# One of six additions of each convolution chunk moved from GpSimd to an accumulating DMA

## The chip, the core and the metric

The kernel runs on one core of a Trainium2 chip. A core has TensorE (matrix products into PSUM), VectorE, ScalarE and GpSimd (element-wise work), SyncE (here it only issues transfers) and 16 DMA engines that all issuers share. The metric is the device time of one execution in microseconds; the profile is of one execution.

## The reference

There are 8 batches of 4224 rows of 192 features. Each row has, for each of 8 heads, 7 raw tap weights. The reference (shortened):

```python
w = exp(weight_gen - max(weight_gen)); w = w / (sum(w) + 1e-9)   # softmax over the 7 taps
out[b, s, h, :] = sum_k w[b, s, h, k] * x_pad[b, s + k, h, :]    # causal, 6 rows of zeros ahead
X = fft(fft(out, axis=1), axis=2)
u = out + real(X)
un = (u - mean(u)) / sqrt(var(u) + 1e-6)
result = u + maximum(un @ w_ch1, 0) @ w_ch2                      # 192 -> 768 -> 192
```

So each batch goes through a dynamic convolution, a two-dimensional Fourier transform whose real part is added, a normalization and a two-layer network.

## The kernel before

The 4224 rows of a batch lie as 128 partitions x 33 row groups. A batch passes through four stages, each a Python generator that issues a little work per step:

- `conv(b)` (lines 306 to 487) computes the convolution in 8 chunks of 4 row groups (128 x 768 values, 384 KB, in f32) and a ninth chunk of one row group. For each chunk, each of the 7 taps gives a product of x and the tap's weight (line 440 on VectorE). The product of the first step (i == 0) is written to the sum `u` itself; the other six go to buffers `pr` (tag `prod`, 5 buffers) and are added to `u` one after the other. From the third batch on all six additions are on GpSimd (lines 448 and 449: `DVE_ADDS` names chunks of the second batch only, and `PE_SUMS` chunks of the first). GpSimd then folds the chunk (L463, L465, tile `sm`), TensorE multiplies it with Fourier tables (L470, `pg`), ScalarE and VectorE make `gt` of that, and SyncE stores it in DRAM (L484, L485, `g_d`).
- `transform(b)` loads `g_d` back (L506, tile `g2`, shown as g) and TensorE makes the second part of the transform (L516, `pp`), which ScalarE copies to `pq`.
- `mix(b, g)` multiplies `pq` with the feature tables (L545, `eo`); VectorE adds the result to `u` (L551 to L555). `norm(b, g)` normalizes a group on ScalarE (L585 to L600, tiles `junk`, `rs`, `un`; a small `rs` step on GpSimd, L598), splits it into a high f16 half (L608, ScalarE) and a low one (L609 and L611, GpSimd), the tile `hl`, and SyncE transposes that by DMA into `ht` (L617).
- `mlp(n)` runs the network for a group: five matmuls for each of six blocks of the hidden layer (L642, `ph`, three PSUM buffers), the rectified result as high and low halves `hh` (L652 on ScalarE, L653 on VectorE), and the second layer (L665, `po`). VectorE adds the residual (L670) and SyncE stores the result (L674).

The stages of different batches overlap: the streams' start and end times in `run()` let the convolution of batch b pass while the network of batch b - 1 and the one before still run. Each engine has one queue and works it in order. The order within a queue is set when the program is built: a planner with a model of the machine takes, on each engine, the work that is ready first, with the program order as priority; `issue_after` adds bounds on it. Once built, an instruction that waits holds everything behind it on its engine. SyncE issues every transfer of this kernel; x has one buffer, so the loads of the next batch (L326) wait for the products of this one.

Buffers matter for the change: a `pr` buffer is free again when the addition that reads it is done.

Of the kernel before, what the change touches and what calls it, by code (L numbers as in the profile page):

```python
# [14 lines left out]
ALU = mybir.AluOpType  # L15
# [21 lines left out]
POOL_TAPS = {(0, 0): (5, 6), (0, 1): (5, 6), (0, 3): (6,), (1, 0): range(7), (1, 1): range(7)}  # L37
DVE_ADDS = {(1, c): 1 for c in range(2, NC)}
F32_GROUPS = 7
ACT_TAPS = {(0, 1): (0,), (0, 3): (0,), (0, 5): (0,1), (0, 7): (0,)}  # L40
TURNS = {1: 'ddpdddd', 2: 'dpddpdd', 3: 'dpddpdp'}
WARM = (20, 0, 12, 12)
# [48 lines left out]
def tile_dynconv_fnet_mlp(  # L91
# [12 lines left out]
    nc = tc.nc  # L104
    B, D = x.shape[0], x.shape[3]
    H, K = wg.shape[3], wg.shape[4]
# [190 lines left out]
    def turns(pool, turn):  # L297

        its = {"p": iter(pool), "d": (k for k in range(K) if k not in pool)}
        return [next(its[t]) for t in turn]  # L300

    def mirrored(ap, step):

        return bass.AP(ap.tensor, ap.offset, [ap.ap[0], [step, 2], *ap.ap[1:]])

    def conv(b):
# [43 lines left out]
        for grp in groups:  # L350
            chunks = []
            wbank = wbanks[b] if b > 0 else pst("wp", 1, [P, 512], F32, f"wp_{b}_{grp[0]}")
            for i, c in enumerate(grp):
                need_x(c)
                need_taps(c)
                R = 4 if c < NC else 1
                on_pe = (b, c) in PE_SUMS
                u = us[b, c] = sb.tile([P, R, D], F32, name=f"u_{b}_{c}",
                                       **(dict(tag="u", bufs=16) if R > 1 else dict(tag="u0", bufs=2)))
# [9 lines left out]
                elif R > 1:  # L369
                    wout = wp.rearrange("p (s n) k -> p s n k", s=2)  # L370
                    nc.vector.tensor_tensor(out=wout, in0=win,
                                            in1=nin.unsqueeze(3).broadcast_to([P, 2, 2 * H, K]), op=ALU.mult)
                else:
                    nc.vector.tensor_tensor(out=wp, in0=w_sb[:, 0:H, :],
                                            in1=ws[:, 0:H].unsqueeze(2).broadcast_to([P, H, K]), op=ALU.mult)
                wq = None
                if len(pt) == K:
                    nc.vector.tensor_tensor(out=win, in0=win, in1=nin.unsqueeze(3).broadcast_to([P, 2, 2 * H, K]),
                                            op=ALU.mult)
                    wq = win  # L380
                elif pt:
                    wq = sb.tile([P, 2, 2 * H, len(pt)], F32, tag="wq", name=f"wq_{b}_{c}", bufs=2)
                    (nc.vector if c > 1 else nc.gpsimd).tensor_tensor(
                        out=wq, in0=win[:, :, :, pt[0]:pt[-1] + 1], in1=nin.unsqueeze(3).broadcast_to([P, 2, 2 * H, len(pt)]), op=ALU.mult)
# [8 lines left out]
            for c, R, u, wp, pa, wq, pt, at in chunks:  # L393
                act_taps = ACT_TAPS.get((b, c), ())
                if act_taps:
                    lo, up, n = 2 * c + 1, N2 - 2 * c - 2, len(act_taps)
                    step = (up - lo) * H
                    wa = sb.tile([P, 2, 2 * H, n], F32, tag="hh", name=f"wa_{b}_{c}", bufs=10)
                    wrows, nrows = w_sb[:, lo * H:(lo + 2) * H, :], ws_of[c][:, lo * H:(lo + 2) * H]
                    nc.vector.tensor_tensor(out=wa, in0=mirrored(wrows, step * K)[:, :, :, act_taps[0]:act_taps[0] + n],  # L400
                                            in1=mirrored(nrows, step).unsqueeze(3).broadcast_to([P, 2, 2 * H, n]), op=ALU.mult)
                for k in act_taps:
                    at[k] = [sb.tile([P, 2, D], F32, tag="hh", name=f"pr_{b}_{c}_{k}_{s}", bufs=10) for s in range(2)]
                    for s in range(2):
                        for j in range(2):
                            for h in range(H):
                                cols = slice(h * G, (h + 1) * G)
                                nc.scalar.mul(at[k][s][:, j, cols], x_sb[:, (up + K - 1 if s else lo) + j + k, cols],
                                              wa[:, s, j * H + h, k - act_taps[0]:k - act_taps[0] + 1])
            for i in range(K):  # L410
                for c, R, u, wp, pa, wq, pt, at in chunks:
                    order = turns(pt, TURNS[len(pt)]) if pt and pa else range(K)
                    order = [k for k in order if k not in at] + list(at)
                    k = order[i]
                    if k in at:
                        for h in range(2):
                            nc.tensor.matmul(pa[h][:, 0:2 * D], lhsT=ident32, rhs=at[k][h].rearrange("p r d -> p (r d)"),
                                             start=(i == 0), stop=(i == K - 1))
                        continue
                    pr = u  # L420
                    if i > 0 or pa:
                        pr = sb.tile([P, R, D], F32, name=f"pr_{b}_{c}_{k}",
                                     **(dict(tag="g2", bufs=3) if b == 0 and pa else dict(tag="prod", bufs=5)))
                    if R > 1:
                        lo, up = 2 * c + 1, N2 - 2 * c - 2 + K - 1
                        rows = mirrored(x_sb[:, lo + k:lo + k + 2, :].rearrange("p r (h g) -> p (r h) g", g=G),
                                        (up - lo) * D)
                        wk = wp[:, :, k:k + 1].rearrange("p (s n) o -> p s n o", s=2)
                        if k in pt:
                            wk = wq[:, :, :, k - pt[0]:k - pt[0] + 1]  # L430
                        wk = wk.broadcast_to([P, 2, 2 * H, G])
                        dst = pr.rearrange("p (s r) (h g) -> p s (r h) g", s=2, g=G)
                    else:
                        rows = x_sb[:, k, :].rearrange("p (h g) -> p h g", g=G)
                        wk = wp[:, :, k:k + 1].broadcast_to([P, H, G])
                        dst = pr.rearrange("p r (h g) -> p (r h) g", g=G)
                    if k in pt:
                        nc.gpsimd.tensor_tensor(out=dst, in0=rows, in1=wk, op=ALU.mult)
                    else:
                        last_product[b] = nc.vector.tensor_tensor(out=dst, in0=rows, in1=wk, op=ALU.mult)  # L440
                    if pa:
                        prf = pr.rearrange("p r d -> p (r d)")
                        n = R * D // 2
                        for h in range(2):
                            nc.tensor.matmul(pa[h][:, 0:n], lhsT=ident32, rhs=prf[:, h * n:(h + 1) * n],  # L445
                                             start=(i == 0), stop=(i == K - 1))
                    elif i > 0:
                        adder = nc.vector if i <= DVE_ADDS.get((b, c), 0) else nc.gpsimd
                        adder.tensor_tensor(out=u, in0=u, in1=pr, op=ALU.add)  # L449
                yield (done + sum(q[1] for q in tails) + sum(q[1] for q in chunks) * i / K) / N2  # L450
            tails += chunks
            while tails and not (b == 1 and grp[0] == 0):
                c, R, u, wp, pa, _, _, _ = tails.pop(0)
# [7 lines left out]
                if R > 1:  # L461
                    sm = sb.tile([P, 2, D], F32, tag="fold", name=f"sm_{b}_{c}", bufs=3)
                    nc.gpsimd.tensor_tensor(out=sm[:, :, 1:D], in0=u[:, 0:2, 1:D], in1=u[:, 3:1:-1, D - 1:0:-1],  # L463
                                            op=ALU.add)
                    last_fold[b] = nc.gpsimd.tensor_tensor(out=sm[:, :, 0], in0=u[:, 0:2, 0], in1=u[:, 3:1:-1, 0],  # L465
                                                           op=ALU.add)
# [155 lines left out]
    def mlp(n):  # L622
# [13 lines left out]
        for c in range(NH):  # L636
            if now:
# [3 lines left out]
                for i, (wt, blk) in enumerate(terms):  # L641
                    last_ph[n] = nc.tensor.matmul(ph[:, 0:T], lhsT=wt[:, cs_], rhs=ht[:, 0:T, blk],  # L642
                                                  start=(i == 0), stop=(i == len(terms) - 1))
                    if i < len(terms) - 1:
                        yield (c + 0.1 * (i + 1)) / NH
                if NG * b + g < F32_GROUPS:
                    a, l = sb.tile([P, 4, P], F32, tag="hh", name=f"hh_{b}_{g}_{c}", bufs=10), None
# [10 lines left out]
            if last:  # L658
                f32 = NG * lb + lg < F32_GROUPS
                per = LT  # L660
# [158 lines left out]
```

## Time and profile before

| | |
|---|---|
| median of 3 runs | 1142.97 us (1142.65 to 1143.59) |
| the profiled execution | 1139.56 us |
| its span, first to last instruction | 1137.8 us |
| mean granted TensorE clock | 0.988 |
| busy: TensorE, VectorE, ScalarE, GpSimd | 1077.1, 972.5, 811.1, 875.2 us |
| additions of line 449 on GpSimd | 396, of these 324 from the third batch on |
| moved by DMA | 128.74 MB, 113 GB/s in the mean |

In the rows PE is TensorE (PEld its weight loads), DVE VectorE, ACT ScalarE, POOL GpSimd and SP SyncE. A group has its busy time in us and the mean duration of one in ns, then the idle time of the engine just before them and what ended it. L449 is line 449 of the kernel. Instructions that issue a DMA do not count as busy. Times inside the execution are counted from the start of the span; in the third batch (b = 2 in the code, which counts from 0) the additions begin at 219 us, and the last batch's end at 961 us.

### The profile page before, as it was taken

Reading aid. Unit: us, or ns where it says so; the run is one execution under the profiler, and the core shown is the slowest. Engines: PE = TensorE matmul, PEld = TensorE weight load, DVE = VectorE, ACT = ScalarE, POOL = GpSimd, SP = SyncE. Lnnn points to the kernel's source line nnn. Section 1 sums busy time; section 2 is a strip of 40 time slices with the busy share of each in tenths; the row PEclk is TensorE's granted clock in tenths of the full one; section 3 lists DMA queues with packets and bytes.
Section 4 is the critical chain, followed back from the end, with each engine's and each line's share of the span. In section 5 each row is a group of like instructions: output and inputs, shape, how many; then the busy total and the mean of one; then the engine's idle time right before and its main releaser. Section 6 shows DMA issues by size and latency. Waiting matters only on the chain.

```text
span 1137.8 us, 23793 instructions
## 1 busy us (share of the span) xinstructions
PE 1077.1 (95%) x8476; PEld 815.0 (72%) x8476; DVE 972.5 (85%) x1825; ACT 811.1 (71%) x2520; POOL 875.2 (77%) x751
## 2 busy tenths in 40 slices
PE   5984999998999999999999999999999999999998
PEld 3454687786677867777778877677777867887777
DVE  7989999889989998999989998999989997356443
ACT  4665676456985799659975899559875898589822
POOL 5979699699978999699969999699959998011200
PEclk9996999999999999999999999999999999999999
DMA  8343344513483148514572347415562234421321
GB/s 304 129 151 98 64 115 134 171 39 113 96 214 103 54 115 228 133 53 120 137 177 81 103 97 216 129 36 129 141 156 60 65 73 98 115 57 46 85 46 47
DMA packets 156504, 128.74 MB, mean 113 GB/s; under 512 B 108571, under 2 KB 133088, under 8 KB 156384
## 3 DMA queue, kind: packets, MB, share of 16 engines
q1 hardware_dynamic: 156384, 127.21, 41.7%
q8 instruction: 67, 1.10, 0.4%
q14 instruction: 53, 0.43, 0.1%
HBM read 61.46 MB, written 39.37 MB: 89 GB/s over the span
## 4 chain that ended last, share of the span: by engine, by line
PE 45%; DVE 17%; ACT 14%; POOL 10%; issue 8%; DMA 5%; SPq 0%; DVEq 0%; POOLq 0%; ACTq 0%
PE ph L642 20%; PE po L665 17%; POOL u L449 7%; DVE pr L440 6%; PE pp L516 4%; ACT junk L589 3%; PE eo L545 2%; ACT junk L585 2%; DVE hh L653 2%; ACT un L600 2%; DMA ht<-hl 2%; ACT hh L652 2%; PE pg L470 1%; PE pa L445 1%; DVE u L440 1%
## 5 line engine op out<-in xcount | busy, mean ns | idle before, releaser
L449 POOL TENSOR_TENSOR u<-u,pr 128x768 f32<-128x768 f32 (+1 forms) x396 | 655.5, 1677 | 67.1 <-DVE pr L440 50.8
L665 PEld LDWEIGHTS <-hh 128*128 128x128 f16 x4248 | 362.7, 98 | 72.2 <-DVE hh L653 2.8
L665 PE MATMUL po<-w2h,hh 128*128 128x192 f16 x2832 | 408.4, 246 | 1.9 <-DVE hh L653 1.8
L642 PE MATMUL ph<-ht,w1h 128*128 128x512 f16 (+1 forms) x1296 | 394.4, 362 | 11.5 <-DMA ht<-hl 9.7
L440 DVE TENSOR_TENSOR pr<-x_sb,wp 128x768 f32<-128x768 f32 (+1 forms) x415 | 354.3, 877 | 14.1 <-POOL u L449 10.0
L665 PE MATMUL po<-w2l,hh 128*128 128x192 f16 x1416 | 345.4, 246 | 0.0
L653 DVE SCALAR_TENSOR_TENSOR hh<-ph,hh 128x512 f16<-128x512 f32 (+1 forms) x390 | 245.8, 636 | 106.4 <-ACT hh L652 105.5
L642 PE MATMUL ph<-ht,w1l 128*128 128x512 f16 (+1 forms) x864 | 310.2, 362 | 0.0
L652 ACT ACTIVATE hh<-ph 128x512 f16<-128x512 f32 (+1 forms) x390 | 213.8, 550 | 130.5 <-PE ph L642 101.7
L642 PEld LDWEIGHTS <-w1h 128*128 128x128 f16 x1296 | 125.5, 98 | 92.6 <-DMA ht<-hl 2.0
L600 ACT ACTIVATE un<-u,rs 128x192 f32<-128x192 f32 x264 | 123.7, 535 | 17.2 <-POOL rs L598 6.7
L642 PEld LDWEIGHTS <-w1l 128*128 128x128 f16 x864 | 85.2, 99 | 61.6 <-issue 11.8
L609 POOL TENSOR_TENSOR hl<-un,hl 128x512 f16<-128x512 f32 (+1 forms) x69 | 74.1, 1075 | 62.0 <-issue 28.8
L589 ACT ACTIVATE junk<-u,rs 128x192 f16<-128x192 f32 x244 | 110.3, 452 | 4.0
L585 ACT ACTIVATE junk<-u 128x192 f16<-128x192 f32 x244 | 88.0, 361 | 19.4 <-DVE u L555 15.9
L520 ACT COPY pq<-pp 97x204 f32<-97x204 f32 (+1 forms) x96 | 47.1, 491 | 58.0 <-PE pp L516 48.7
L545 PE MATMUL eo<-cs_sb,pq 97*128 97x97 f32 x544 | 82.4, 275 | 5.6 <-DVE u L555 5.6
L545 PEld LDWEIGHTS eo<-cs_sb,pq 97*128 97x128 f32 x544 | 76.7, 193 | 11.2 <-issue 6.9
L670 DVE SCALAR_TENSOR_TENSOR u<-po,isc,u 128x384 f32<-128x384 f32 (+1 forms) x122 | 72.6, 596 | 7.5 <-PE po L665 7.5
L463 POOL TENSOR_TENSOR sm<-u 128x382 f32<-128x382 f32 x64 | 65.6, 1025 | 5.0 <-ACT u L458 4.9
L665 PE MATMUL po<-w2f,hh 128*128 128x192 f32 x336 | 62.4, 327 | 0.0
L665 PEld LDWEIGHTS po<-w2f,hh 128*128 128x128 f32 x336 | 56.0, 190 | 4.6 <-PE pg L470 0.2
(111 smaller groups left out, 1265.4 us busy)
## 6 DMA issues: line engine op xcount, KB each, us to landing
out_dram<-u SPq DMA_DIRECT2D x64, 384.0 KB
x_sb<-in_x_dram SPq DMA_DIRECT2D x48, 384.0 KB
g<-g_d SPq DMA_DIRECT2D x40, 336.0 KB
x_sb<-in_x_dram SPq DMA_DIRECT2D x8, 864.0 KB
g_d<-gt SPq DMA_DIRECT2D x32, 195.0 KB
g_d<-gt SPq DMA_DIRECT2D x32, 189.0 KB
w<-in_weight_gen_dram SPq DMA_DIRECT2D x6, 924.0 KB
x_sb<-in_x_dram SPq DMA_DIRECT2D x8, 672.0 KB
```

Source lines behind the costliest of these rows:

```text
L440: last_product[b] = nc.vector.tensor_tensor(out=dst, in0=rows, in1=wk, op=ALU.mult)
L449: adder.tensor_tensor(out=u, in0=u, in1=pr, op=ALU.add)
L545: nc.tensor.matmul(eo[:, e, j, :], lhsT=pq[0:DH, e, r, r:r + P], rhs=cs_sb[:, e, :], start=True, stop=True)
L585: nc.scalar.activation(junk, uv[:, t, :], AF.Identity, accum_out=st[:, t, 0:1])
L589: nc.scalar.activation(junk, uv[:, t, :], AF.Square, bias=rs[:, 2, t:t + 1], accum_out=st[:, t, 1:2])
L600: nc.scalar.activation(halves[t // 2][:, t % 2, :], uv[:, t, :], AF.Identity, bias=rs[:, 1, t:t + 1], scale=rs[:, 0, t:t + 1])
L609: lo_eng.tensor_tensor(out=hl[:, t0:t1, 2 * P:3 * P], in0=src[:, 0:t1 - t0, 0:P], in1=hl[:, t0:t1, 0:P], op=ALU.subtract)
L642: last_ph[n] = nc.tensor.matmul(ph[:, 0:T], lhsT=wt[:, cs_], rhs=ht[:, 0:T, blk], start=(i == 0), stop=(i == len(terms) - 1))
L652: nc.scalar.activation(a[:, 0:T], ph[:, 0:T], AF.Relu)
L653: nc.vector.scalar_tensor_tensor(out=l[:, 0:T], in0=ph[:, 0:T], scalar=0.0, in1=a[:, 0:T], op0=ALU.max, op1=ALU.subtract)
L665: nc.tensor.matmul(po[t // 2][:, t % 2, :], lhsT=hx[:, t], rhs=wx[:, c2, :], start=(c2 == 0 and i == 0), stop=(c2 == NH - 1 and i == len(t ...
L670: nc.vector.scalar_tensor_tensor(out=lt, in0=po[t // 2][:, 0:t % 2 + 1], scalar=scales[0][:, 1:2] if f32 else isc, in1=lt, op0=ALU.mult, o ...
```

## The change

From the third batch on (`DMA_SUMS = 2`), in the eight chunks of four row groups, the products of steps 1 and 2 are no longer added to `u` as they come. They are kept as a pair, and when the second is there GpSimd issues a DMA that reads the second product and adds it to the first, in place, SBUF to SBUF (128 x 768 f32, 384 KB). At the last step, before the last product is added, GpSimd adds the pair's sum to `u`. So a chunk has five additions on GpSimd and one DMA where it had six additions. The ninth chunk and the first two batches are as before.

```diff
+DMA_SUMS = 2
...
+            pair = {}
             for i in range(K):
                 for c, R, u, wp, pa, wq, pt, at in chunks:
...
+                    elif R > 1 and b >= DMA_SUMS and i in (1, 2):
+                        pair.setdefault(c, []).append(pr)
+                        if i == 2:
+                            first, second = pair[c]
+                            nc.gpsimd.dma_start(first, second, accum_op=ALU.add)
                     elif i > 0:
+                        if c in pair and i == K - 1:
+                            nc.gpsimd.tensor_tensor(out=u, in0=u, in1=pair.pop(c)[0], op=ALU.add)
                         adder = nc.vector if i <= DVE_ADDS.get((b, c), 0) else nc.gpsimd
                         adder.tensor_tensor(out=u, in0=u, in1=pr, op=ALU.add)
```

## The prediction

> **What bounds the kernel now.** I read first the page's busy shares, then the chain that ended last.
>
> ```profile
> PE 1077.1 (95%) x8476; PEld 815.0 (72%) x8476; DVE 972.5 (85%) x1825; ACT 811.1 (71%) x2520; POOL 875.2 (77%) x751
> ...
> PE 45%; DVE 17%; ACT 14%; POOL 10%; issue 8%; DMA 5%; SPq 0%; DVEq 0%; POOLq 0%; ACTq 0%
> ```
>
> These are averages over stages, so the second view is the busy time by stretch: from the first addition of the third batch (b=2, about 219 us) to the last addition of the eighth (961 us), then one batch period, then ten busy microseconds of DMA. Columns: stretch, length, busy time of PE, PEld, DVE, ACT, POOL (with instruction counts), granted clock, DMA share, GB/s.
>
> ```profile
> 214.00:961.00 747.00, 726.88 (x6080) 558.03 (x6079) 698.63 (x1267) 571.57 (x1761) 680.04 (x576) 1.00 0.44 114
> 466.00:592.00 126.00, 124.44 (x1059) 95.80 (x1058) 119.79 (x212) 97.86 (x303) 113.97 (x97) 1.00 0.46 124
> 440.00:450.00 10.00, 10.00 (x83) 7.46 (x82) 7.87 (x22) 9.81 (x32) 8.88 (x9) 1.00 1.07 301
> ```
>
> Over the six changed batches TensorE is idle for 747 - 726.88 = 20.1 us, VectorE for 48.4 (8.1 a batch), GpSimd for 67.0 (11.2 a batch). A modelled busy time may hide gaps, so I checked TensorE by pace. One period holds these matmuls (470 to 596 us), and their paces come from the longest stretches of the chain:
>
> ```profile
> L665 PE MATMUL po<-w2h,hh 128*128 128x192 f16 x403 | 58.3, 246 | 0.0
> L665 PE MATMUL po<-w2l,hh 128*128 128x192 f16 x202 | 49.3, 246 | 0.0
> L642 PE MATMUL ph<-ht,w1h 128*128 128x512 f16 (+1 forms) x162 | 49.2, 361 | 0.0
> L642 PE MATMUL ph<-ht,w1l 128*128 128x512 f16 (+1 forms) x108 | 38.7, 361 | 0.0
> L545 PE MATMUL eo<-cs_sb,pq 97*128 97x97 f32 x68 | 9.9, 273 | 0.5 <-DVE u L555 0.5
> L470 PE MATMUL pg<-sm,f_sb 128*128 128x192 f32 x32 | 6.7, 332 | 0.0
> L516 PE MATMUL pp<-te_sb,g 102*97 102x102 f32 (+1 forms) x44 | 4.9, 252 | 1.1 <-DMA g<-g_d 1.1
> L516 PE MATMUL pp<-to_sb,g 102*97 102x102 f32 (+1 forms) x44 | 4.8, 250 | 0.0
> ```
>
> ```profile
> 417.11 0.68 PE pg L470 x4
> ...
> 601.31 1.40 PE pp L516 x16
> ...
> 1040.08 1.12 PE eo L545 x10
> ...
> 1062.65 2.16 PE ph L642 x10
> ...
> 1132.35 2.49 PE po L665 x30
> ```
>
> ```profile
> 515.38 0.22 PE L642 MATMUL ph<-ht,w1h 128*128 128x128 f16 x1
> 515.43 0.22 PE L642 MATMUL ph<-ht,w1l 128*128 128x128 f16 x1
> ```
>
> po: 605 x 0.083 = 50.2 us. ph: 240 wide ones x 0.216 = 51.8, and the 30 of the one-row group at 0.05 = 1.5. eo: 68 x 0.112 = 7.6. pg: 34 (two more than the row, for the chunk of row 0) x 0.17 = 5.8. pp: 88 x 0.0875 = 7.7. Together 124.6 of 126 us. TensorE really issues back to back, and a batch cannot go much under 125 us whatever GpSimd does. The ceiling of any gain here is the 20.1 us of idle TensorE, less what GpSimd has no part in. Its waits in that stretch:
>
> ```profile
> PE ph L642 <- DMA ht<-hl: 8.9, 8, 3.8
> PE pp L516 <- DMA g<-g_d: 5.7, 5, 2.0
> ```
>
> The first is the only one with GpSimd close behind it: L609 and L611 make the low halves of hl and the transpose L617 follows them. Two of the eight waits, 3.8 and 1.0 us, lie in batch 2's convolution and are not GpSimd's: it stood idle before the hl of the longer one, as its queue shows; the other is in TensorE's own line.
>
> ```profile
> 280.12 1.16 POOL L609 TENSOR_TENSOR hl<-un,hl 128x512 f16<-128x512 f32 x1 [0.41 <-ACT gt L475]
> ```
>
> ```profile
> 265.86 0.38 PE L642 MATMUL ph<-ht,w1h 128*128 128x512 f16 x1 [1.05 <-DMA ht<-hl]
> ```
>
> At 774 us the hl came behind additions. First the chain there, then GpSimd's queue ahead of it:
>
> ```profile
> 772.54 1.16 POOL hl L609
> ...
> 774.97 6.09 DMA ht<-hl
> ```
>
> ```profile
> 765.28 1.82 POOL L449 TENSOR_TENSOR u<-u,pr 128x768 f32<-128x768 f32 x1
> ...
> 767.21 5.37 POOL L449 TENSOR_TENSOR u<-u,pr 128x768 f32<-128x768 f32 x3
> ```
>
> **The change part by part.** In each of 6 x 8 = 48 chunks one addition of L449 leaves GpSimd, and one DMA is issued from its queue. Three additions in 5.37 us, the last shown to its full 1.82 us, give (5.37 - 1.82) / 2 = 1.78 us apart. Removed: 8 x 1.78 = 14.2 us of GpSimd a batch.
>
> Added is an issue on GpSimd. The trace has no DMA from that queue, so it is bounded by SyncE's issues:
>
> ```profile
> L326 SPq DMA_DIRECT2D x_sb<-in_x_dram x80: 327/360/1388, 1.7 to 828.3; - x80
> ...
> L617 SPq DMA_TRANSPOSE ht<-hl x72: 1190/1454/5139, 113.4 to 1100.0; - x72
> ```
>
> 0.33 us is the lower end (a plain row-wise copy of as many bytes); 5.14 us, the longest transpose, is the far upper one. An accumulation is no plain copy, and I take 1.1 us, an estimate near the transpose's 1.19 to 1.45. GpSimd then has -14.2 + 8 x 1.1 = -5.4 us a batch (-11.6 at 0.33, -2.6 at 1.45, +26.9 at 5.14). No queue of SyncE is passed; the DMA joins GpSimd's queue only.
>
> The DMA must land before the pair sum (first of the two additions at i == 6). Three additions cover it: 3 x 1.78 = 5.3 us. Landings of similar transfers in the chain:
>
> ```profile
> 407.30 4.07 DMA ht<-hl
> ...
> 442.38 4.38 DMA x_sb<-in_x_dram
> ...
> 464.87 3.54 DMA g_d<-gt
> ```
>
> With 774.97 above: 3.54 us for half the bytes, 4.38 for an x load while the DMA engines were full (share 1.07), 4.07 and 6.09 for SBUF to SBUF. The change reads two operands, so the far upper bound is twice the longest, 12.2 us. I take 5.0, about the mean of the two SBUF-to-SBUF rows: under 5.3, so no wait. If that cover is gone, each microsecond over 5.3 stops GpSimd. Behind the waiting addition stand u + pr6, the fold L463/L465, hl and the small rs of the norm; pg, the transposes and ScalarE's un wait for those. The Trainium skill ("DMA: Bandwidth & Descriptors", Anatomy of one DMA) puts a GpSimd-issued DMA at 2.0 us plus bytes/436e3, here 2.9 us, and 3.8 if both operands count; by it the sum stays as it is and rival 2 below has next to no chance. The landings in the rows are longer than that, and the chances below go by the rows.
>
> The buffers of tag prod (5) are held longer: pr1 until i == 6, pr2 until the landing. VectorE runs at most five products ahead now, and three while a pair is open. Its wait for them now is small:
>
> ```profile
> DVE pr L440 <- POOL u L449: 4.2, 8, 0.8
> ```
>
> I add nothing for it (0 to +12 us, third rival). At a batch's start the first work on u comes two products later; GpSimd's idle time there hides it. Its queue at the start of one batch (b = 4), and the products:
>
> ```profile
> 470.71 13.10 POOL L449 TENSOR_TENSOR u<-u,pr 128x768 f32<-128x768 f32 x7 [8.33 <-DVE pr L440]
> ```
>
> ```profile
> L440 DVE TENSOR_TENSOR pr<-x_sb,wp 128x768 f32<-128x768 f32 (+1 forms) x415 | 354.3, 877 | 14.1 <-POOL u L449 10.0 <-DMA x_sb<-in_x_dram 2.2 <-PE pa L445 1.5
> ```
>
> Uncovered it would cost two products, 2 x 0.9 us, a batch.
>
> More DMA traffic: 8 x 384 KB = 3.1 MB a batch on top of 124 GB/s x 126 us = 15.6 MB, a fifth more (two fifths if both reads count). One transpose a batch that is waited for and takes a fifth of 5 us longer is +1 us a batch at worst; I take +1 us over the whole run, as most transposes have time in hand (8 waits for 52), with bounds 0 and +6.
>
> What reaches the end of GpSimd's relief: of the 8.9 us, 4.1 remain without the two waits named. I take half, -2.0 (bounds -4.1 and 0): an hl still waits for whatever addition is in front of it. The planner orders each queue anew, which I cannot read from the trace; I give it +-4 us, a fifth of the 20.1 us of idle either way, and 0 in the sum. **Sum: -2.0 + 1.0 = -1.0 us.** The profiled execution took 1139.56 us (span 1137.8 and 1.8 around it) and would take 1138.6; the median of the runs is 3.4 us higher, so 1142. One more row, for the rivals:
>
> ```profile
> POOL hl L609 <- ACT hl L608: 12.6, 8, 5.0
> ```
>
> **The rivals.** (1) The relief goes through: all 4.1 us of hl waits end, and two thirds of the 5.7 us for g as the convolutions end sooner: -7.9, 1135 us. For it: GpSimd is 91% busy and stands in the chain. Against: g waits for the last chunks of a batch, and near them GpSimd already waits for ScalarE (the row above, 12.6 us), more than TensorE waits for hl.
>
> (2) Slower: the pair sum waits for the landing, at the head of GpSimd's in-order queue. Net per chunk: -0.68 + (landing - 5.3). It decides from 11.2 / 8 = 1.4 us net, a landing of 7.4 us; then GpSimd overtakes TensorE. With two operands at the mean of the two shortest landings, 3.54 and 4.07, 7.6 us: 1.62 x 8 - 11.2 = 1.8 us a batch, 11 over six, 1154. At 2 x 4.38 it is 66 us, 1209. For it: two reads, full DMA engines when x is loaded; against: the single rows.
>
> (3) VectorE runs short of prod buffers and its queue stops with hh behind it. It decides at 8.1 / 8 = 1.0 us a chunk; at 1.25 us it is (10 - 8.1) x 6 = 11 us, 1154. Against: its wait is 4.2 us now, and TensorE has three ph banks.
>
> (4) The change does not do what it says: the issue costs GpSimd what an addition did (1.78 us), nothing moves, 1143 us.
>
> **How the numbers follow.** About 0.2% (2.3 us) is what a measurement of this kernel can tell from no change. Forecast 0.48, its own range 1137 to 1148 (the +-4 us of order): faster 0.14, same 0.22, slower 0.12. Rival 1: 0.20, faster. Rival 2: 0.17 and rival 3: 0.10, slower. Rival 4: 0.05, same. So faster 0.34, same 0.27, slower 0.39. The range takes in rival 1 and the nearer ends of rivals 2 and 3: 1134 to 1159.
>
> **What would show it.** GpSimd's additions in the stretch now:
>
> ```profile
> L449 POOL TENSOR_TENSOR u<-u,pr 128x768 f32<-128x768 f32 (+1 forms) x324 | 538.2, 1685 | 51.8 <-DVE pr L440 48.5
> ```
>
> Right: 324 - 48 = 276 additions on GpSimd there, 48 of them the pair sums' new line, TensorE still under 25 us idle there, GpSimd's idle time up by 0 to 12 us a batch, the pair's addition hardly waiting for a DMA. Rival 2 would show as GpSimd waiting at the pair addition for a DMA, rival 3 as VectorE's L440 waiting for one. Wrong at the root would be a TensorE idle time after 219 us that moves by more than 10 us, or periods other than 125 to 127 us.

## The result, and the profile after

| | before | after |
|---|---|---|
| median | 1142.81 us | 1208.01 us (1205.47 to 1209.81) |
| ratio | | 1.0569, 95% interval 1.0547 to 1.0592 |
| the profiled execution | 1139.56 us, span 1137.8 | 1209.81 us, span 1208.0 |
| mean granted TensorE clock | 0.988 | 0.963 |

The change costs 65 us, far outside the predicted range. New line numbers: the products are L442, the additions L458, the pair's addition L456, the DMA L453, `hh` L661 and L662, the first layer L651, the second L674, `pp` L525, `pg` L479.

The page of the changed kernel has these busy shares and this chain that ended last:

```profile
PE 1104.7 (91%) x8476; PEld 830.4 (69%) x8476; DVE 973.2 (81%) x1825; ACT 807.1 (67%) x2520; POOL 837.6 (69%) x751
...
PE 38%; DVE 18%; POOL 14%; ACT 11%; DMA 11%; issue 8%; SPq 1%; DVEq 0%; POOLq 0%; ACTq 0%
```

The stretch of the six changed batches, in the columns of the prediction:

```profile
214.00:961.00 747.00, 691.11 (x5617) 527.21 (x5616) 655.08 (x1174) 516.84 (x1591) 605.11 (x534) 0.97 0.57 132
```

GpSimd did get its relief: over the whole run its busy time falls from 875.2 to 837.6 us, which is 6.3 us for each of the six batches (the prediction had 5.4). Its idle time in the stretch is 747 - 605 = 142 us, 67 before. But TensorE, busy for all but 20.1 us before, now idles 55.9 us, and less gets done (5617 matmuls in these 747 us, 6080 before). Of the 70.2 us between the two profiled spans, 27.6 are busy time of TensorE (1104.7 against 1077.1 for the same 8476 matmuls, at the lower clock) and 42.6 are its idle time. What stops first is VectorE. The waits of the changed kernel (engine, line waited for: us in total, times, longest):

```profile
DVE pr L442 <- DMA pr<-pr: 24.9, 11, 8.9
DVE u L442 <- DMA out_dram<-u: 24.8, 11, 5.7
PE ph L651 <- DVE hh L662: 22.0, 12, 5.7
PE pp L525 <- DMA g<-g_d: 13.8, 7, 4.6
...
POOL u L456 <- DMA pr<-pr: 8.6, 2, 6.1
PE ph L651 <- DMA ht<-hl: 8.2, 3, 5.4
```

VectorE's products wait 24.9 us for landings, that is for a product buffer, and another 24.8 us for stores of the output, that is for a `u` buffer; neither wait is in the profile of before. The products themselves are no slower beside the transfers (944 ns for a wide one, 946 before). Behind them in VectorE's queue stand the low halves `hh`, for which TensorE now waits 22.0 us. The kernel before had this row:

```profile
PE ph L642 <- DVE hh L653: 0.9, 2, 0.7
```

GpSimd itself hardly waits for the landing (8.6 us, two times). GpSimd's groups and the DMA's row (its last number is the median time from issue to landing in us):

```profile
L458 POOL TENSOR_TENSOR u<-u,pr 128x768 f32<-128x768 f32 (+1 forms) x300 | 507.3, 1719 | 30.2 <-DVE u L458 12.3 <-DVE pr L442 10.4 <-PE pa L447 0.2
L456 POOL TENSOR_TENSOR u<-u,pr 128x768 f32<-128x768 f32 x48 | 88.9, 1852 | 10.9 <-DMA pr<-pr 8.6
L453 POOL DMA_DIRECT2D pr<-pr x48 | 42.9, 893 | 51.6 <-DVE pr L442 46.0 <-DMA g_d<-gt 2.7 <-DVE bn L588 1.9
```

```profile
pr<-pr POOLq DMA_DIRECT2D x48, 384.0 KB, 4.2
```

So the change does what it says. An issue is recorded at 0.89 us and a landing at 4.2 us in the median, both under what the prediction took. The longest stop shows the rest: first the chain, then VectorE's and TensorE's queues, then the stretch of 20 us around it, after and before, and last the six microseconds behind the stop.

```profile
318.92 13.25 DMA pr<-pr
...
332.20 0.95 DVE pr L442
```

```profile
332.20 0.95 DVE L442 TENSOR_TENSOR pr<-x_sb,wp 128x768 f32<-128x768 f32 x1 [8.88 <-DMA pr<-pr]
```

```profile
334.23 1.62 PE L479 MATMUL pg<-sm,f_sb 128*128 128x192 f32 x4 [6.32 <-DVE u L564]
```

```profile
320.00:340.00 20.00, 13.68 (x93) 9.57 (x91) 10.21 (x30) 12.33 (x45) 11.64 (x12) 0.83 1.10 191
```

```profile
320.00:340.00 20.00, 20.00 (x161) 14.26 (x159) 17.29 (x28) 17.50 (x43) 15.08 (x21) 1.00 0.80 212
```

```profile
332.00:338.00 6.00, 3.77 (x14) 2.80 (x15) 5.80 (x18) 3.76 (x16) 3.16 (x4) 0.50 0.83 265
```

One landing takes 13.25 us while the DMA engines are full (share 1.10). VectorE has no product buffer for 8.88 of them; TensorE's queue stands at `pg`, which waits for VectorE's work behind that product; and the granted clock of the stretch falls to 0.83, with 0.50 in the six microseconds from 332 us on. The Trainium skill ("TensorE: Matmul & The Clock Gate", The HAM clock gate) says that the array runs at half clock after an idle window of about 3.4 us; the clock of 0.50 behind a stop of 6.32 us agrees with that. So the lost time is more than the waits alone.

Late in the run the other wait does the same. The periods between the transforms of successive batches, 123.4 to 126.5 us before from the second transform on, are between 119.6 and 147.0 us now. The longest runs from the first matmuls of the seventh batch's transform to those of the eighth's:

```profile
895.42 0.59 PE L525 MATMUL pp<-te_sb,g 102*97 102x102 f32 x4 [1.19 <-DMA g<-g_d]
```

```profile
1042.42 0.87 PE L525 MATMUL pp<-te_sb,g 102*97 102x102 f32 x8
```

Inside it a product waits for a store that was issued at 969.03 us and landed 8.48 us later:

```profile
977.60 0.95 DVE L442 TENSOR_TENSOR u<-x_sb,wp 128x768 f32<-128x768 f32 x1 [5.69 <-DMA out_dram<-u]
```

### The profile page after: what moved, and what is told of

The parts are those of the page before. It is cut to its first block, busy times and chain, and to the rows that moved or that the text cites. A ratio compares the mean times of both kernels' runs of the same rounds, so it can differ in the third digit from the quotient of the medians.

```text
span 1208.0 us, 23886 instructions
## 1 busy us (share of the span) xinstructions
PE 1104.7 (91%) x8476; PEld 830.4 (69%) x8476; DVE 973.2 (81%) x1825; ACT 807.1 (67%) x2520; POOL 837.6 (69%) x751
## 4 chain that ended last, share of the span: by engine, by line
PE 38%; DVE 18%; POOL 14%; ACT 11%; DMA 11%; issue 8%; SPq 1%; DVEq 0%; POOLq 0%; ACTq 0%
PE ph L651 17%; PE po L674 14%; POOL u L458 9%; DVE pr L442 7%; PE pp L525 4%; DMA pr<-pr 3%; DMA out_dram<-u 3%; DVE hh L662 2%; ACT un L609 2%; ACT hh L661 2%; POOL u L456 2%; ACT junk L594 2%; ACT junk L598 2%; PE eo L554 2%; DMA ht<-hl 1%
## 5 line engine op out<-in xcount | busy, mean ns | idle before, releaser
L458 POOL TENSOR_TENSOR u<-u,pr 128x768 f32<-128x768 f32 (+1 forms) x300 | 507.3, 1719 | 30.2 <-DVE u L458 12.3
L651 PE MATMUL ph<-ht,w1h 128*128 128x512 f16 (+1 forms) x1296 | 404.2, 368 | 31.2 <-DVE hh L662 22.0
L674 PE MATMUL po<-w2h,hh 128*128 128x192 f16 x2832 | 417.7, 247 | 11.1 <-DVE u L679 4.6
L674 PEld LDWEIGHTS <-hh 128*128 128x128 f16 x4248 | 366.3, 99 | 86.3 <-issue 9.8
L442 DVE TENSOR_TENSOR pr<-x_sb,wp 128x768 f32<-128x768 f32 (+1 forms) x415 | 349.9, 875 | 37.5 <-DMA pr<-pr 24.9
L674 PE MATMUL po<-w2l,hh 128*128 128x192 f16 x1416 | 346.7, 247 | 0.0
L662 DVE SCALAR_TENSOR_TENSOR hh<-ph,hh 128x512 f16<-128x512 f32 (+1 forms) x390 | 244.3, 633 | 123.8 <-ACT hh L661 123.1
L661 ACT ACTIVATE hh<-ph 128x512 f16<-128x512 f32 (+1 forms) x390 | 214.1, 552 | 170.1 <-PE ph L651 145.5
L651 PE MATMUL ph<-ht,w1l 128*128 128x512 f16 (+1 forms) x864 | 315.1, 368 | 0.0
L651 PEld LDWEIGHTS <-w1h 128*128 128x128 f16 x1296 | 127.7, 100 | 96.1 <-issue 7.8
L618 POOL TENSOR_TENSOR hl<-un,hl 128x512 f16<-128x512 f32 (+1 forms) x69 | 77.5, 1123 | 110.6 <-ACT hl L617 74.2
L651 PEld LDWEIGHTS <-w1l 128*128 128x128 f16 x864 | 86.0, 100 | 80.5 <-issue 35.3
L456 POOL TENSOR_TENSOR u<-u,pr 128x768 f32<-128x768 f32 x48 | 88.9, 1852 | 10.9 <-DMA pr<-pr 8.6
L453 POOL DMA_DIRECT2D pr<-pr x48 | 42.9, 893 | 51.6 <-DVE pr L442 46.0
L607 POOL TENSOR_TENSOR rs<-rs 128x4 f32<-128x4 f32 (+1 forms) x61 | 15.3, 259 | 90.8 <-DVE rs L601 44.1
```

The lines of the kernel that those rows point to most:

```text
L456: nc.gpsimd.tensor_tensor(out=u, in0=u, in1=pair.pop(c)[0], op=ALU.add)
L618: lo_eng.tensor_tensor(out=hl[:, t0:t1, 2 * P:3 * P], in0=src[:, 0:t1 - t0, 0:P], in1=hl[:, t0:t1, 0:P], op=ALU.subtract)
L661: nc.scalar.activation(a[:, 0:T], ph[:, 0:T], AF.Relu)
L662: nc.vector.scalar_tensor_tensor(out=l[:, 0:T], in0=ph[:, 0:T], scalar=0.0, in1=a[:, 0:T], op0=ALU.max, op1=ALU.subtract)
L674: nc.tensor.matmul(po[t // 2][:, t % 2, :], lhsT=hx[:, t], rhs=wx[:, c2, :], start=(c2 == 0 and i == 0), stop=(c2 == NH - 1 and i == len(t ...
```

## The experiments

**First round: which wait.** The theory at this point is that the products wait for the landing (L). Its rivals are that the traffic disturbs the other transfers (C), that the new order of adding costs without any transfer (O), and that the `u` buffers come round before their stores (U).

In the first run GpSimd makes the pair's sum itself, so there are six additions again:

```diff
-                            nc.gpsimd.dma_start(first, second, accum_op=ALU.add)
+                            nc.gpsimd.tensor_tensor(out=first, in0=first, in1=second, op=ALU.add)
```

> The changed kernel with one edit: the pair is summed by an addition on GpSimd in the DMA's place (the same two products, kept as long, no DMA; GpSimd again has six additions a chunk). Theory L (VectorE's queue stops because a prod buffer is held until the DMA lands): 1140 to 1155 us, VectorE's wait for prod buffers under 12 us and no wait for a DMA there. Rival C (the added traffic slows the other transfers): the same, 1140 to 1155. Rival O (the new order of the queues and the pair's longer hold alone cost the time, whoever adds): 1190 to 1215. Rival U (the u buffers come round before the results are stored): 1180 to 1200, with VectorE's wait for the stores of u still near 25 us.

1157.27 us, ratio 1.0131 (1.0110 to 1.0152). That is just above what L and C expected and far below O and U; no product waits for a store here. The pairs cost some 15 us without a transfer, and the other 50 us need the DMA or what follows from it. One of these things is a new order: the planner plans every kernel of this round anew.

The next two are the changed kernel with more product buffers, and with more `u` buffers:

```diff
-**(dict(tag="g2", bufs=3) if b == 0 and pa else dict(tag="prod", bufs=5)))
+**(dict(tag="g2", bufs=3) if b == 0 and pa else dict(tag="prod", bufs=7)))
```

> The changed kernel with seven prod buffers instead of five. To make room the Fourier table has 9 of its 17 rows and the second half of the first weights takes the place of the first half, so the output isn't the reference's; the work is the same. Theory L: 1140 to 1170 us, VectorE's wait for the accumulating DMA under 6 us instead of 24.9. Rivals C and O: 1195 to 1215. Rival U: 1185 to 1205, its wait for the stores of u as long as before or longer.

```diff
-**(dict(tag="u", bufs=16) if R > 1 else dict(tag="u0", bufs=2)))
+**(dict(tag="u", bufs=18) if R > 1 else dict(tag="u0", bufs=2)))
```

> The changed kernel with eighteen u buffers instead of sixteen, and the same room made as in prod7 (the output isn't the reference's; the work is the same). Rival U: 1140 to 1170 us, VectorE's wait for the stores of u under 5 us instead of 24.8. Theory L: 1180 to 1205, the wait for the accumulating DMA still over 15 us. Rivals C and O: 1195 to 1215.

1199.65 us (1.0507; 1.0487 to 1.0527) with seven product buffers, 1184.74 us (1.0380; 1.0348 to 1.0413) with eighteen `u` buffers. Each takes its own wait away and leaves the other, the first in U's range (C's and O's have it too) and the second in L's. VectorE's waits with seven product buffers, then with eighteen `u` buffers, where no wait for a store is left:

```profile
DVE u L443 <- DMA out_dram<-u: 27.9, 23, 3.8
...
DVE pr L443 <- DMA pr<-pr: 3.7, 3, 1.9
```

```profile
DVE pr L443 <- DMA pr<-pr: 33.2, 19, 9.2
```

The queues as written out say why. On VectorE's queue, between the residual addition after which a `u` buffer is stored and the product that writes it two batches later, stand 40 to 73 instructions in the fifth to eighth batches of the kernel before. In the changed kernel this falls from batch to batch, to 2 to 21 in the eighth; with seven product buffers it is down to 2 to 32 in the fifth already. So the planner puts the convolution, now cheaper for GpSimd, ever further ahead, until only the `u` buffers hold it. It also means that neither run is the changed kernel with one buffer count changed alone: each has an order of its own.

The last run of this round is the kernel before with 48 accumulating DMAs into a tile that nobody reads:

```diff
                     elif i > 0:
+                        if R > 1 and b >= 2 and i == 2:
+                            nc.gpsimd.dma_start(spare.rearrange("p r d -> p (r d)"), f1_sb[:, 0:6, :].rearrange("p r k -> p (r k)"), accum_op=ALU.add)
```

> The kernel before with all six additions, and in the same 48 chunks an accumulating DMA of the same size from GpSimd (a table onto a spare tile) whose result nobody uses or waits for, but the next such DMA. To make room the Fourier table has 9 of its 17 rows, read over again, so the output isn't the reference's; the work is the same. Theory L: 1143 to 1158 us (0.9 us of issue in 48 chunks on GpSimd, hidden mostly). Rival C: 1180 us or more, with the waits of TensorE for ht and g at twice those of before. Rivals O and U: 1140 to 1155.

1210.76 us (1.0619; 1.0584 to 1.0654), but it answers another question: nothing held these DMAs in place, all of them were issued between 19 and 357 us, and GpSimd waits at 14 of them for the landing of the one before.

```profile
POOL spare L452 <- DMA spare<-f_sb: 41.0, 14, 6.3
```

The loss is in the first batches (periods 163.6 and 148.5 us; 121.6 to 127.6 after that). The run decides nothing here; the DMAs stand in their places in two runs below.

**Second round: is it the planner's order?** Theory P says that the order costs, not the transfer.

In the first run the DMA is left out and the rest of the change kept:

```diff
                         pair.setdefault(c, []).append(pr)
-                        if i == 2:
-                            first, second = pair[c]
-                            nc.gpsimd.dma_start(first, second, accum_op=ALU.add)
```

> The changed kernel with the DMA left out: the second product of the pair is made but never added, so the output is not the reference's; GpSimd has the five additions of the changed kernel and no transfer. The order that is written into the queues is again one in which the convolution runs far ahead: in the fifth to eighth batches only 2 to 9 of VectorE's instructions stand between the residual addition that frees a u buffer and the product that writes it from the fourth chunk on (40 to 60 in the kernel before, 2 to 35 in the changed one). Theory P (the planner's order is what costs: with cheaper additions it lets the convolution run ahead until only the u buffers hold it) expects 1180 to 1215 us although no transfer is left, with VectorE's u products waiting for the stores of the output by over 15 us. Theory L (the products wait for the accumulating DMA's landing) and rival C (the transfer's traffic) both expect 1143 us or less (1128 to 1145), as GpSimd has 14 us less work a batch and nothing is waited for.

1199.36 us (1.0518; 1.0486 to 1.0550): less work, no transfer, and nearly the whole loss, with VectorE waiting for stores, as P expected.

```profile
DVE u L442 <- DMA out_dram<-u: 26.2, 19, 2.5
```

An order can cost this much by itself. Whether that of the changed kernel does is another matter. The next two runs keep its DMAs and hold the convolution back:

```diff
+                    elif i == 0 and R > 1 and b >= 2:
+                        with tc.issue_after(last_res[NG * (b - 2) + c + 2].ins):
+                            nc.vector.tensor_tensor(out=dst, in0=rows, in1=wk, op=ALU.mult)
...
+                        last_res[NG * lb + lg] = nc.vector.scalar_tensor_tensor(out=lt, in0=po[t // 2][:, 0:t % 2 + 1],
```

> The changed kernel with its 48 DMAs, and one bound more on the order: from the third batch on the first product of a chunk (b, c) stands on VectorE's queue behind the last residual addition of group c + 2 of batch b - 2, so that 43 to 69 instructions lie between a u buffer's release and its next use, as in the kernel before (40 to 73). Theory P expects the loss to go: 1135 to 1157 us, no VectorE wait for stores and TensorE idle in all by less than 75 us. Theory L and rival C, whose transfers are all still there, expect 1185 to 1215 us, with VectorE's products still waiting 15 to 30 us for landings.

> As the run with the held convolution, but each chunk's first product stands behind the residual of group c + 3 instead of c + 2 (53 to 91 instructions between release and next use). Theory P expects it near the run with c + 2, within 12 us either way (1135 to 1160); if the run with c + 2 is still short of room, this one is the faster of the two. Theory L and rival C expect 1185 to 1215 us.

1169.88 us (1.0256; 1.0238 to 1.0275) and 1172.45 us (1.0280; 1.0263 to 1.0298). Neither side's figure: in the first of them 38 of the 65 us go, 27 stay. The store waits are gone in both. VectorE's landing waits stay in the first and are small in the second, which is no faster (214 to 1000 us):

```profile
DVE pr L445 <- DMA pr<-pr: 24.4, 12, 8.9
```

```profile
DVE pr L445 <- DMA pr<-pr: 7.0, 10, 1.8
```

So the sum of one wait is not its price: in the second run TensorE waits 19.0 us for `hh`, 11.5 in the first.

The last run of this round has the unneeded DMAs in place, behind the second addition of each chunk:

```diff
+                        added = adder.tensor_tensor(out=u, in0=u, in1=pr, op=ALU.add)
+                        if R > 1 and b >= 2 and i == 2:
+                            with tc.issue_after(added.ins):
+                                nc.gpsimd.dma_start(spare.rearrange("p r d -> p (r d)"), f1_sb[:, 0:6, :].rearrange("p r k -> p (r k)"), accum_op=ALU.add)
```

> The kernel before, all six additions kept, plus 48 accumulating DMAs of 384 KB from a table into a tile that nobody reads, each issued on GpSimd's queue right behind the second addition of its chunk (so the traffic and the issues of the changed kernel in their places, without a reader that waits and without relief for GpSimd). The Fourier table is shortened to make room, so the output is not the reference's. GpSimd has 48 issues of about 0.9 us more, 43 us in all or 7 a batch of the 11 it has idle. Rival C (traffic delays transposes and loads) expects 1185 us or more. Theories P and L expect 1143 to 1158 us: the traffic itself costs little, with landings of 4 to 6 us in the median.

1197.45 us (1.0513; 1.0483 to 1.0543): as rival C expects, TensorE waits for transposes. But the planner had made a new order here too, so order and transfer are still mixed.

```profile
PE ph L648 <- DMA ht<-hl: 31.8, 9, 10.2
```

Its GpSimd queue shows what an issue takes there, and a trap:

```profile
541.47 0.84 POOL L455 DMA_DIRECT2D spare<-f_sb  x1
542.08 2.07 POOL L452 TENSOR_TENSOR u<-u,pr 128x768 f32<-128x768 f32 x1
543.84 0.46 POOL L604 TENSOR_TENSOR rs<-rs 128x4 f32<-128x4 f32 x1
```

From start to start the issue takes 0.61 us and the addition behind it 1.76, the pace of before, although the addition is recorded at 2.07 us: behind this DMA issue the records overlap. A mean duration of GpSimd's records can so grow without a loss of pace.

**Third round: the order held.** Each engine's queue is now written out in full: every instruction is tied behind its neighbour in an order taken from another kernel, so that two kernels differ in the transfer alone.

```diff
     run()
+    for name, places in ORDER.items():
+        row = [traced[name][p] for p in places]
+        for one, two in zip(row, row[1:]):
+            tc.add_manual_dep(two, one.name, mybir.DependencyInfo(
+                mybir.DependencyClass.NoSync, mybir.DependencyReason.DATA), reason="order")
```

> The changed kernel, DMAs, pair sums and all, but with every engine's queue written out in the order of the kernel before (each instruction tied behind its neighbour; on GpSimd the DMA stands where the second addition stood, the pair's addition right ahead of the last one). Theory P (what costs is the order that the planner makes, not the transfer) expects 1135 to 1152 us. Theory L (landings hold the product buffers) expects VectorE's products to wait 15 us or more for landings and 1165 us or more; rival C (traffic) expects 1185 us or more. Both P and L may hold in part: between 1152 and 1185 the landing wait of VectorE says how much is L's.

> The kernel with five additions and no transfer (the second product of the pair is left out of the sum, so the output is not the reference's), every queue in the order of the kernel before. GpSimd has 14 us a batch less to do and nothing new to wait for. Theory P expects 1130 to 1143 us, that is 55 us and more below the same work in the planner's own order (1199 us). If the order does not matter, it stays near 1199 us. The difference to the run with the DMA in the same order is the price of the transfer alone.

> The same work without a transfer (the second product is left out of the sum), but every queue in the order of the changed kernel, with only the 48 DMAs taken out of it. Theory P expects the loss to stay: 1180 to 1210 us. Theories L and C, which put the loss on the transfer, expect 1150 us or less.

> The kernel before with all six additions and 48 accumulating DMAs into a tile that nobody reads, each behind the second addition of its chunk, every queue in the order of the kernel before (the Fourier table is shortened to make room, so the output is not the reference's). GpSimd's start-to-start time for an issue was 0.6 us in the run with the planner's order: 8 x 0.6 = 5 us a batch of its 11 idle. Theory P expects 1142 to 1158 us, against 1197 us in the planner's order; rival C expects 1185 us or more again, with TensorE waiting over 20 us for the transposes.

| | order of before | order of the change |
|---|---|---|
| five additions, no transfer | 1157.60 (1.0135; 1.0115 to 1.0155) | 1165.06 (1.0205; 1.0189 to 1.0222) |
| the change, with transfer | 1231.10 (1.0766; 1.0736 to 1.0796) | 1208.01 (1.0569; 1.0547 to 1.0592) |
| six additions and an unneeded transfer | 1177.63 (1.0309; 1.0292 to 1.0326) | |

Theory P falls for this change: in the order of before it is slower still, and in its own order the same work without the transfer loses only 23 us, of which 7 are the order's (1165.06 - 1157.60). The transfer, with the buffer that it holds, costs 43 us in the one order and 73 in the other. Of these runs only that with the transfer in the order of before lies where L and C had it. Without the transfer P expected 1130 to 1143 us in the order of before and 1180 to 1210 in that of the change, and L and C 1150 or less in the latter; neither run came out so. Where the transfer's time went in the order of before is plain from VectorE's waits (214 to 1000 us):

```profile
DVE pr L442 <- DMA pr<-pr: 43.6, 21, 5.2
DVE pr L442 <- POOL u L456: 34.2, 19, 4.6
DVE pr L442 <- POOL u L458: 23.5, 17, 2.6
```

```profile
PE ph L651 <- DVE hh L662: 47.2, 26, 5.0
```

Products wait for the second buffer of the pair (the landing), for the first (the pair's addition) and for the other additions: 101 us in all, and TensorE waits 47 us for `hh`. This is the prediction's third rival. Without the transfer only the first product is kept, and these waits are 33 us:

```profile
DVE pr L442 <- POOL u L455: 19.4, 15, 2.6
DVE pr L442 <- POOL u L453: 14.0, 9, 3.3
```

The unneeded transfer costs 36 us in the same order, less than C expected and more than P. It holds no product buffer. The issues come on top of six additions on GpSimd here, and products wait 31.2 us for additions (4.2 before); TensorE waits 15.6 us for transposes (8.9 before). How the 36 us divide between the two was not measured.

```profile
DVE pr L443 <- POOL u L452: 31.2, 54, 1.7
```

```profile
PE ph L648 <- DMA ht<-hl: 15.6, 7, 4.8
```

**Fourth round: buffers or transfer.** Theory B says that the held buffers cost, T that the transfer itself does. The first two runs have the order of before and seven product buffers, with and without the change; the next two have six, with one `u` buffer less, in the order of before and in the planner's own.

```diff
-dict(tag="prod", bufs=5)
+dict(tag="prod", bufs=7)
...
-dict(tag="prod", bufs=5)
+dict(tag="prod", bufs=6)
-dict(tag="u", bufs=16)
+dict(tag="u", bufs=15)
```

> The changed kernel in the queues' order of the kernel before, with seven product buffers instead of five: as many free ones as before while a pair is open. (Room for them: nine of seventeen Fourier tables are kept, and the second half's weights of the first layer share the tiles of the first half's, so the output is not the reference's; the instructions are the same.) Theory B (the pair holds two of the five product buffers, VectorE's queue stops at the next product, hh comes late and TensorE waits) expects 1135 to 1157 us instead of 1231, with VectorE's waits for landings and for the pair's addition falling from 80 us to under 15. Theory T (the transfer itself disturbs: traffic, the landing, its issue) expects 1185 us or more.

> The kernel before in its own order with the same seven product buffers and the same shared tables and weights: what the room and the two more buffers do by themselves. Both theories expect 1130 to 1146 us (VectorE waits for product buffers 4 us in all in the kernel before, so there is next to nothing to win). If it is well below 1142, the run with the DMA is to be compared with this one.

> The changed kernel, its full computation, in the order of the kernel before, with six product buffers and fifteen u buffers instead of sixteen. Theory B expects it between five and seven product buffers: 1150 to 1195 us, VectorE's waits for landings and pair additions about half of the 80 us; the u buffer that is missing costs nothing in this order, which leaves 40 places on VectorE's queue between release and next use (24 a group). Theory T expects 1200 us or more.

> The same buffers (six for products, fifteen for u), the order left to the planner. With one u buffer less the convolution cannot run as far ahead in the plan: 29 to 66 places stay between a u buffer's release and its next use up to the last batch (2 to 21 in the changed kernel). Theory P with theory B (run-ahead in the plan and the held buffers share the loss) expects 1150 to 1185 us, near the held order's 1170. Theory T expects 1185 us or more.

| the change in the order of before | time | ratio |
|---|---|---|
| 5 product buffers | 1231.10 | 1.0766 (1.0736 to 1.0796) |
| 6 (and 15 `u` buffers) | 1183.36 | 1.0365 (1.0330 to 1.0401) |
| 7 | 1169.62 | 1.0245 (1.0209 to 1.0280) |
| the kernel before, 7 | 1141.08 | 0.9998 (0.9987 to 1.0009) |

Both B and T hold in part: 61 of the 89 us go with two more buffers (VectorE's landing wait falls from 43.6 to 6.0 us), 28 stay, and the kernel before gains nothing from them. The run with six has a share of store waits in it (6.9 us), as it has one `u` buffer less.

```profile
DVE pr L443 <- DMA pr<-pr: 6.0, 6, 2.1
```

With six buffers and the planner's order it is 1182.30 us (1.0357; 1.0333 to 1.0382), the upper end of what P and B together expected: its landing waits are small, its store waits are not:

```profile
DVE u L442 <- DMA out_dram<-u: 18.1, 13, 2.9
...
DVE pr L442 <- DMA pr<-pr: 7.0, 6, 2.3
```

What stays at seven buffers is seen in TensorE's waits from 214 to 1000 us and in the stretch, each with the DMA first and then in the kernel before with seven buffers:

```profile
PE ph L652 <- DMA ht<-hl: 17.9, 9, 3.9
PE ph L652 <- DVE hh L663: 6.6, 8, 1.3
```

```profile
PE ph L643 <- DMA ht<-hl: 8.8, 7, 3.8
PE pp L517 <- DMA g<-g_d: 6.0, 6, 2.1
...
PE ph L643 <- DVE hh L654: 0.9, 3, 0.4
```

```profile
214.00:961.00 747.00, 713.02 (x5882) 544.00 (x5881) 679.14 (x1222) 551.84 (x1689) 616.52 (x548) 0.98 0.58 136
```

```profile
214.00:961.00 747.00, 728.23 (x6065) 558.91 (x6064) 697.08 (x1265) 572.15 (x1764) 676.15 (x568) 0.99 0.44 114
```

TensorE waits 9 us longer for transposes in all and 6 us longer for `hh`; the DMA share is 0.58 for 0.44.

**Last: is the rest the transfer's, by its bytes?** The last two runs have the same order and seven buffers, one without the transfer (the second product is left out of the sum) and one with half of each transfer:

```diff
-                            nc.gpsimd.dma_start(first, second, accum_op=ALU.add)
+                            nc.gpsimd.dma_start(first[:, 0:2], second[:, 0:2], accum_op=ALU.add)
```

> Five additions on GpSimd and no transfer (the second product of the pair is left out of the sum, and as before the Fourier tables and weights are shared, so the output is not the reference's), seven product buffers, the order of the kernel before. Theory B with T (the 28 us that seven buffers leave are the transfer's own price) expects 1128 to 1146 us. If it stays at 1155 us or more, the rest is not the transfer's, but the relief's or the held buffer's.

> The run with seven product buffers and the DMA in the order of the kernel before (1170 us), but each DMA adds only the first half of the 768 columns (192 instead of 384 KB; the other half of the second product is left out of the sum). If the rest of the loss goes by the bytes that the DMA engines move beside the transposes, it expects 1150 to 1161 us, about half of the 28 us, with TensorE waiting 10 to 15 us for transposes (17.9 with the whole, 8.8 without). If it goes by the number of transfers or by their issue on GpSimd, 1163 to 1172 us.

1146.37 us (1.0045; 1.0028 to 1.0062) without, 1157.55 us (1.0139; 1.0093 to 1.0184) with half, 1169.62 us with the whole: 11 us for 48 x 192 KB and 23 us for 48 x 384 KB. For a price by the number of issues the expectation was 1163 to 1172 us with half of each, and 1157.55 us (some 5 us to either side) lies just below that; so the price goes roughly by the bytes. TensorE's wait for transposes steps with it (6.5, 11.6 and 17.9 us). VectorE's wait for landings does so too (none, 2.8 and 6.0 us), so the 23 us are the whole transfer's price, and not that of its traffic alone. With half, then without:

```profile
PE ph L652 <- DMA ht<-hl: 11.6, 8, 4.0
```

```profile
PE pp L523 <- DMA g<-g_d: 8.4, 6, 2.4
PE ph L649 <- DMA ht<-hl: 6.5, 5, 3.8
PE ph L649 <- DVE hh L660: 6.2, 9, 1.3
```

Of the versions that keep the transfer and compute everything, the fastest is the first with the convolution held back, 1169.88 us; none came near the kernel before.

## Why the prediction was wrong, step by step

- **TensorE's ceiling of 20.1 us.** Nothing contradicts it: no run beat the kernel before beyond the noise, not even the one without a transfer and with seven product buffers (1146 us).
- **GpSimd's relief, -2.0 us.** The row it was taken from moved as forecast: with five additions, no transfer and seven buffers TensorE waits 6.5 us for transposes instead of 8.8. But the waits for `g` (8.4 for 6.0) and `hh` (6.2 for 0.9) grew by more, and that kernel is 5 us slower than the one before with seven buffers. The relief was worth nothing; why `hh` comes later there stays open.
- **The issue, 1.1 us.** It is recorded at 0.89 us, and the one shown from start to start takes 0.61. That is right in kind, and the halved transfers show no price that goes by the number of issues.
- **The landing, 5.0 us, under a cover of 5.3.** The median is 4.2 us, and GpSimd at the pair's addition waits 8.6 us in all; rival 2 did not come. That its far case (two reads at 4.38 us) gave 1209 us, next to the measured 1208, is luck: it wanted GpSimd to wait for every landing. The Trainium skill ("DMA: Bandwidth & Descriptors", Anatomy of one DMA) gave estimates of 2.9 or 3.8 us: the median is above both, and the 13.25 us of one landing far above. The cover was worked out for GpSimd alone. VectorE waits for a landing too, as the second product's buffer is free only then; the prediction says so ("pr2 until the landing") and gives that wait no cover and no time.
- **"I add nothing for it (0 to +12 us, third rival)".** This is the step that failed, a term put at nothing. In the order of before the held buffers cost 61 us (1231 with five, 1170 with seven). The rival's rule came near that: it decides at a wait of 1.0 us a chunk, VectorE's waits of 101 us over 48 chunks are 2.1 us a chunk, and (2.1 - 1.0) x 48 = 53 us. What was wrong is the evidence against it, "its wait is 4.2 us now": a wait of 4.2 us with five free buffers says nothing on the wait with three.
- **"I take +1 us over the whole run ... with bounds 0 and +6".** The term was mis-sized: where the buffers suffice, the transfer still costs 23 us (1169.62 - 1146.37), 0.5 us for each 384 KB, with VectorE's landing waits of 6.0 us in it. Most transposes do have time in hand: TensorE waits for 9 of them with the transfer and for 5 without. But those 9 waits are 2.0 us each and the 5 are 1.3, 11.4 us more in all, and the two profiled executions are 14.7 us apart (1163.93 and 1149.19). The bound of +6 took one late transpose a batch, and 1 us for it.
- **"I give it +-4 us ... and 0 in the sum".** The orders differ by more: the same additions without a transfer take 1158 us in the order of before, 1165 us in that of the change, and 1199 us in the order that the planner makes for them. For the change as timed the new order is no loss (1208 against 1231 us in the old one), but a held convolution in the same buffers takes 1170 us.

How the 65 us of the changed kernel divide follows in part only. 23 are there in its own order without the transfer; of these 16 are there in the order of before as well, and 11 of the 16 go with two more buffers. 43 come with the transfer. If 23 of these are what the transfer costs in the held order with seven buffers, 20 are left for the buffers that it holds; that split was not measured in the changed kernel's own order, and stays open. So does the price of the store waits. With 18 `u` buffers they are gone and the kernel is 23 us faster, but the planner also made a new order for it; in the changed kernel's order without the transfer there are 14.0 us of them in a run that loses 23.

## What to carry to other kernels

Work that was moved to a DMA had three prices here beside its issue: the bytes, paid by the transfers that someone waits for; the buffers, held from the operand's making to the landing and the last reader; and the order that a planner makes of the cheaper engine. Count how many buffers are left while one is held, and do not read the slack of a pool from the waits of a kernel in which none is held. To tell these prices apart, hold every queue's order and change one of them.

## What was not expected of the hardware

Six batches with eight 384 KB transfers each raise the DMA share from 0.43 to 0.58 only, and still cost 23 us; at half the bytes the share is 0.52 and the price 11 us. One accumulating transfer of 384 KB lands after 4.2 us in the median and after 13.25 us in a stretch with a DMA share of 1.10, where x is loaded. In the held order with seven buffers the median is 4.5 us, and 3.5 for half the bytes. And the clock counts: TensorE's 8476 matmuls took 27.6 us more busy time, at a mean granted clock of 0.963 for 0.988, though none of them was changed; behind the longest stop the clock was 0.50 for six microseconds.
